# A four-layer transformer kernel: a planner with measured wake-up times, a table of priority offsets, and a bias row with a 128-row operand

## The chip, the cores and the metric

The kernel runs on one core of a Trainium2 chip. The metric is the device time of one execution in microseconds (us). Before the change it is 555.64 us, the median of 3 runs (554.33 to 561.57). The profiled execution has a span of 551.9 us.

## What is computed

Two attention layers and two MLP layers alternate on one sequence of 2048 tokens with 512 channels. Attention has 32 heads of 16 channels and a causal sliding window of 256 tokens.

```
def _A_ref(x, wqkv, wo):                       # H = 32, Dh = 16, W = 256
    q, k, v = split(x @ wqkv)
    scores = q @ k^T * Dh ** -0.5
    mask = (i - j >= 0) & (i - j < W)
    p = softmax(where(mask, scores, -1e9))
    return (p @ v) @ wo
def _B_ref(x, w1, b1, w2, b2):                 # F = 1792
    return gelu(x @ w1 + b1) @ w2 + b2
x = A_x
x = x + _A_ref(layernorm(x), A_wqkv, A_wo)
x = x + _B_ref(layernorm(x), B_w1, B_b1, B_w2, B_b2)
x = x + _A_ref(layernorm(x), A_wqkv, A_wo)
x = x + _B_ref(layernorm(x), B_w1, B_b1, B_w2, B_b2)
```

## The kernel before

**Order.** Nothing is ordered by hand. The builder hands some thousands of operations to a planner, class `_Plan` (L168). `add` (L180) takes an operation's engine, its estimated duration, the names that it reads and writes, a priority (smaller goes first), the PSUM banks that it takes or frees, and, for some, an alternative engine. `run` (L207) then plays the program through on estimated times. At each moment an engine that is free takes the ready operation with the smallest priority whose banks can be had. The order found so is written out as one fixed queue per engine; the waits are added by `_Sched.op` (L62). On the chip every engine works through its queue in that order. If the plan was wrong on when something is ready, the engine stands at it, and what is behind it stands too.

The planner's times have three parts. The first is the duration of each operation, given where it is added: `d_psum`, `d_bf2`, `d_act`, `mm` (L390 to L400) and single numbers. The second is `LAT` (L172), the time from the end of an operation to the moment at which another engine can start on its result; it depends only on the engine that produced it. The third is the time for which a DMA holds its issuing queue on SyncE (`issue`, kept in `geo`), beside the time to its landing. PE pays 98 ns whenever the form of its tiles changes (L294).

**Work.** The two attention layers together give 16 blocks of 256 tokens (`NB`, L845). For each block:
- `layernorm` (L522): statistics on DVE (L530, L532), the reciprocal root on Pool (L534, L537), the normalised row `xn` on DVE (L540), its transposes on PE (L548) and an evacuation (L517 on DVE or L519 on ACT).
- `lnq` and `kv`: projections to Q, K and V. All full-size matmuls go through `pe_group`, so that they share one line, L564.
- `attention`: ten visits. `visit` computes scores into four PSUM banks (L665), in tiles of 32 rows by 64 columns, and ACT takes the exp of each pair of banks (L678). `mask` multiplies the edges of the window with 0 and 1, on DVE (L689) or on Pool (L692). `pv` multiplies with V (L726), four times a block.
- Normalisation, after each `pv`: DVE reduces PSUM to OD (L737). A chain of DMAs on SyncE's queue follows: the denominators go to Dc (L741), DVE takes reciprocals (L744), they go to DRAM (L746) and come back broadcast as Rn (L748); four more copies shift rows of OD (L751). Then OT = OD x Rn on Pool (L754) or DVE (L757). There are 64 such chains with seven DMAs each.
- `outproj`: OT times Wo, then the sum into the stream X (L573).
- `mlp` (L800): the two matmuls of the MLP for a job of two or four tiles of tokens, put in beside later blocks. The bias b1 comes in on DVE (L814) or inside ACT's gelu (L826); ACT reloads its table when it goes between exp and gelu. The bias b2 is the first matmul of each output group (L833): a one-row operand of ones times the row b2, added into PSUM.

**PSUM.** Eight banks are shared by classes of use: scores `sc` take four banks from six possible sets, `o` (projections and the like) one of banks 6 and 7, `od` two banks, `m1` any one.

The last attention block's exps end at about 512 us; the rest of the span is the last jobs of the MLP.

Of the kernel before, what the change touches and what calls it, by code (L numbers as in the profile page):

```python
# [7 lines left out]
ALU = mybir.AluOpType  # L8
# [159 lines left out]
class _Plan:  # L168
# [3 lines left out]
    LAT = {"pe": 230.0, "act": 110.0, "dve": 110.0, "pool": 150.0, "sp": 100.0}  # L172
# [7 lines left out]
    def add(self, eng, fn, dur, reads=(), writes=(), prio=0.0, alloc=None, free=(), after=(), geo=None, table=None, dma=False, alt=(), war=()):  # L180


        i = len(self.nodes)
        deps = set(after)
        for r in reads:
            if r in self.lw:
                deps.add(self.lw[r])
        for w in tuple(writes) + tuple(war):
            if w in self.lw:
                deps.add(self.lw[w])  # L190
            deps.update(self.lr.get(w, ()))
        for r in reads:
            self.lr.setdefault(r, []).append(i)
        for w in writes:
            self.lw[w] = i
            self.lr[w] = []
        deps.discard(i)
        if free and eng == "dve":
            prio -= 1000.0
        self.nodes.append(dict(  # L200
            eng=eng, fn=fn, dur=dur, reads=list(reads), writes=list(writes), prio=prio,
            alloc=alloc, free=tuple(free), deps=deps, geo=geo, table=table, dma=dma,
            alts=((eng, fn, dur, 0.0),) + tuple(alt), done=False,
        ))
        return i

    def run(self):  # L207
# [13 lines left out]
        efree = {e: 0.0 for e in engs}  # L221
        last_geo = [None]
# [16 lines left out]
        while left:  # L239
# [9 lines left out]
            for e in engs:  # L249
                while pend[e] and pend[e][0][0] <= t + 1e-9:  # L250
                    _, i = heapq.heappop(pend[e])
                    for a in nodes[i]["alts"]:
                        if a[0] == e:
                            heapq.heappush(ready[e], (nodes[i]["prio"] + a[3], i))
                if efree[e] > t + 1e-9 or not ready[e]:
                    continue
                skipped = []
                pick = None
                while ready[e]:
                    p, i = heapq.heappop(ready[e])  # L260
                    nd = nodes[i]
                    if nd["done"]:
                        continue
                    if nd["alloc"] is not None:
                        cls, groups = nd["alloc"]
                        got = None
                        for c in self.pools[cls]:
                            if all(bank_free[b] for b in c):
                                got = c
                                break  # L270
                        if got is None:
                            skipped.append((p, i))
                            continue
                        pos = 0
                        for g, k in groups:
                            gmap[g] = got[pos : pos + k]
                            pos += k
                        for b in got:
                            bank_free[b] = False
                    pick = i  # L280
                    break
                for s in skipped:
                    heapq.heappush(ready[e], s)
                if pick is None:
                    continue
                nd = nodes[pick]
                nd["done"] = True
                for a in nd["alts"]:
                    if a[0] == e:
                        nd["eng"], nd["fn"], nd["dur"] = a[:3]  # L290
                dur = nd["dur"]
                if e == "pe":
                    if last_geo[0] is not None and last_geo[0] != nd["geo"]:
                        dur += 98.0  # L294
                    last_geo[0] = nd["geo"]
                if nd["table"] is not None:
                    if last_tab[0] != nd["table"]:
                        dur += 1283.0
                    last_tab[0] = nd["table"]
                nd["start"] = t  # L300
                busy[e] += dur
                end = t + dur
                lat = self.LAT[e]
                if e == "sp":
                    efree[e] = t + nd["geo"]
                else:
                    efree[e] = end
                heapq.heappush(events, (efree[e], pick, None))
                order.append(pick)
                left -= 1  # L310
                for g in nd["free"]:
                    heapq.heappush(events, (end + 90.0, n + seq, gmap[g]))
                    seq += 1
                for s in succ[pick]:
                    same = len(nodes[s]["alts"]) == 1 and nodes[s]["eng"] == e
                    r = end if same and e == "pe" else end + (60.0 if same else lat)
                    if r > rtime[s]:
                        rtime[s] = r
                    indeg[s] -= 1
                    if indeg[s] == 0:  # L320
                        for a in nodes[s]["alts"]:
                            heapq.heappush(pend[a[0]], (rtime[s], s))
                        heapq.heappush(events, (rtime[s], n + seq, None))
                        seq += 1
# [3 lines left out]
        return order  # L328


def bass_interleave_layers__sliding_block__dense_activation_gelu__prompt_kernel(
# [48 lines left out]
    POOL_M = 1120.0  # L380
# [9 lines left out]
    def d_psum(n):  # L390
        return n * 1.042 + 150

    def d_bf2(n):
        return n * 0.52 + 200

    def d_act(n):
        return n * 0.833 + 65
# [4 lines left out]
    with ExitStack() as kctx:  # L402
        S_ = _Sched(nc, kctx)

        def sb(name, shape, dtype=dt.bfloat16):
# [6 lines left out]
        onesb = sb("onesb", [P, P])  # L412
        zerob = sb("zerob", [P, VW])
        b2row = sb("b2row", [P, D])
        b1T = sb("b1T", [P, FC], dt.float32)
# [28 lines left out]
            "sc": [(0, 1, 2, 3), (4, 5, 0, 1), (2, 3, 4, 5), (6, 7, 0, 1), (2, 3, 6, 7), (4, 5, 6, 7)],  # L444
# [35 lines left out]
        add("pool", lambda e, B: e.memset(onesb[:], 1.0), 150, writes=["onesb"])  # L480
        add("pool", lambda e, B: e.memset(Va[:, :, :, Dh:VW], 1.0), 600, writes=["V%d" % i for i in range(VR)])

        for h in range(2):
            add("dve", lambda e, B, h=h: e.memset(ps[:, 4 * h : 4 * h + 4, :], 0.0), 2200, writes=["ps:init%d" % h], prio=-200)
# [30 lines left out]
        def evac(dst, src, n, reads, writes, prio, free=(), after=(), two=False, kind="", boot=False):  # L515

            return add("dve", lambda e, B: e.tensor_copy(dst(B), src(B)), 420 if two else d_psum(n),  # L517
# [5 lines left out]
        def layernorm(tau, layer, dst, dcol, dname, prio):  # L523
# [6 lines left out]
            add("dve", lambda e, B: e.bn_stats(stat6[:, k6, :], X[:, t, :]), 680,  # L530
                reads=["X%d" % t], writes=["st%d" % k6], prio=prio)
            add("dve", lambda e, B: e.bn_aggr(statmv[:, k, :], stat6[:, k6, :]), 150,  # L532
                reads=["st%d" % k6], writes=["mv%d" % k], prio=prio)
            add("pool", lambda e, B: e.tensor_scalar(  # L534
                out=veps[:, k : k + 1], in0=statmv[:, k, 1:2], scalar1=EPS, scalar2=None, op0=ALU.add), 250,
                reads=["mv%d" % k], writes=["ve%d" % k], prio=prio - 500)
            add("pool", lambda e, B: e.tensor_tensor(  # L537
                out=rstd[:, k : k + 1], in0=veps[:, k : k + 1], in1=mhalf[:], op=ALU.pow), 590,
# [3 lines left out]
                op0=ALU.subtract, op1=ALU.mult), 400,  # L542
# [58 lines left out]
        def kv(b, prio, vprio):  # L601
# [3 lines left out]
            for i in range(DC // 2):  # L605
# [5 lines left out]
                    in1=parmask[:, :, None].to_broadcast([P, 2, 512]), op=ALU.mult), d_psum(1024) + 60,  # L611
# [22 lines left out]
        def attention(b, prio):  # L634
# [11 lines left out]
            def visit(g):  # L646
# [12 lines left out]
                def sc(e, B):  # L659
# [11 lines left out]
                    "pe", sc, 512 / 2.4 + 30.0 * len(pieces), reads=rd,  # L671
# [12 lines left out]
            def mask(u, n):  # L684
# [4 lines left out]
                add("dve", lambda e, B: e.tensor_tensor(out=Ew, in0=Ew, in1=Mw, op=ALU.mult), d_bf2(8 * HK * n),  # L689
# [4 lines left out]
            def pv(c):  # L694
# [20 lines left out]
                def fn(e, B):  # L715
# [15 lines left out]
                dpv = 2 * sum(max(q[i][3] - q[i][2] for q in seq if i < len(q)) * HK / 2.4 + 14.0 for i in range(max(len(q) for q in seq)))  # L731
# [11 lines left out]
                    ["Dc%d" % rs], reads=ods, prio=pr - 50, dur=2200.0, issue=580.0)  # L743
                add("dve", lambda e, B: e.reciprocal(Rc[:, rs, :], Dc[:, rs, :]), 330,  # L744
                    reads=["Dc%d" % rs], writes=["Rc%d" % rs], prio=pr - 800)
                dma(lambda e, B: e.dma_start(scr_r[rs].rearrange("h (k n) -> (h k) n", n=32), Rc[:, rs, :]),  # L746
                    ["SR%d" % rs], reads=["Rc%d" % rs], prio=pr - 50, dur=2000.0, issue=490.0)
                dma(lambda e, B: e.dma_start(Rn[:, rs, :], scr_r[rs][:, None, :].to_broadcast([HC, Dh, 2 * P])),  # L748
                    ["Rn%d" % rs], reads=["SR%d" % rs], prio=pr - 50, dur=3200.0, issue=580.0)
                for r in range(RG):  # L750
                    dma(lambda e, B, r=r: e.dma_start(  # L751
                        OD[32 * r + Dh : 32 * r + 2 * Dh, s, 0, :], OD[32 * r : 32 * r + Dh, s, 1, :]),
                        [ods[r]], reads=["Dc%d" % rs], prio=pr, dur=2200.0, issue=350.0)
                add("pool", lambda e, B: e.tensor_tensor(  # L754
                    out=OT[:, bs, c, :], in0=OD[:, s, 0, :], in1=Rn[:, rs, :], op=ALU.mult), 750,
                    reads=ods + ["Rn%d" % rs], writes=["OT%d_%d" % (bs, c)], prio=pr,
                    alt=(("dve", lambda e, B: e.tensor_tensor(  # L757
                        out=OT[:, bs, c, :], in0=OD[:, s, 0, :], in1=Rn[:, rs, :], op=ALU.mult), 420, 0.0),))
# [41 lines left out]
        def mlp(J, live, prio1, prio2):  # L800
# [7 lines left out]
            for f0 in range(0, npre, PG):  # L808
                fcs = range(f0, min(f0 + PG, npre))
                for fc in fcs:  # L810
# [8 lines left out]
                    d_act(M * len(fcs)) + 90, reads=["g%d" % fc for fc in fcs], writes=["g%d" % fc for fc in fcs], prio=prio1,  # L819
                    table="gelu", after=gate_act)  # L820
            for fc in range(npre, FC):
# [6 lines left out]
                    d_act(M) + 90, reads=["ps:" + g, "b1T"], writes=["g%d" % fc], prio=prio1, free=[g],  # L828
                    table="gelu", after=gate_act)
            for i in range(n):  # L830
                tau = tau0 + i
                g = "y%d" % tau
                pe_group(g, [(onesb[0:1, :], b2row[0:1, :], slice(0, 512), True, False)] + [  # L833
# [19 lines left out]

        order = PL.run()
# [46 lines left out]
```

The softmax here doesn't subtract the row's maximum and nothing guards it: scores larger than these inputs give would overflow.

## Time and profile before

| engine | busy, us | share of the span |
|---|---|---|
| TensorE (PE) | 484.1 | 88% |
| ScalarE (ACT) | 423.6 | 77% |
| VectorE (DVE) | 385.9 | 70% |
| GpSimd (POOL) | 271.1 | 49% |

How to read the views. A line of a group or a wait names the engine and the line of the code (L564 is line 564). "A <- B: us, times, longest" in the list of waits says that A's engine was idle until B had finished. In the timeline a row gives start, time, engine and operation, and in brackets the idle time ahead of it with its releaser. PEld is the loading of weights, which runs beside PE; SPq is SyncE's queue, which issues the DMAs. PE's ends are modelled, so PE can be called busy while it drains. The costliest groups are the 320 exps (303.6 us on ACT), the 163 masks on Pool (192.1 us), 448 matmuls of the MLP's second half (120.2 us) and 64 reductions to OD on DVE (77.9 us).

### The profile page before, as it was taken

Reading aid. Unit: us, or ns where it says so; the run is one execution under the profiler, and the core shown is the slowest. Engines: PE = TensorE matmul, PEld = TensorE weight load, DVE = VectorE, ACT = ScalarE, POOL = GpSimd, SP = SyncE. Lnnn points to the kernel's source line nnn. Section 1 sums busy time; section 2 is a strip of 40 time slices with the busy share of each in tenths; the row PEclk is TensorE's granted clock in tenths of the full one; section 3 lists DMA queues with packets and bytes.
Section 4 is the critical chain, followed back from the end, with each engine's and each line's share of the span. In section 5 each row is a group of like instructions: output and inputs, shape, how many; then the busy total and the mean of one; then the engine's idle time right before and its main releaser. Section 6 shows DMA issues by size and latency. Waiting matters only on the chain.

```text
span 551.9 us, 20560 instructions
## 1 busy us (share of the span) xinstructions
PE 484.1 (88%) x9040; PEld 247.1 (45%) x9040; DVE 385.9 (70%) x669; ACT 423.6 (77%) x507; POOL 271.1 (49%) x359
## 2 busy tenths in 40 slices
PE   3895788989878997998998999998999998969997
PEld 2553454545433542545444453445434443434653
DVE  5997986868687666856788686786766675863331
ACT  2788798889877894798869987589757996788542
POOL 6575664646584335643566457562553344532010
PEclk9998799999979997998999999999999999979999
DMA  8901111010111011100111101110111102110100
GB/s 275 297 17 41 43 27 40 23 34 20 36 45 33 14 25 38 37 24 11 37 35 33 30 14 42 34 29 15 45 53 43 32 9 61 45 45 25 51 20 30
DMA packets 37131, 24.93 MB, mean 45 GB/s; under 512 B 16305, under 2 KB 36530, under 8 KB 37042
## 3 DMA queue, kind: packets, MB, share of 16 engines
q1 hardware_dynamic: 37042, 23.62, 14.6%
q8 instruction: 71, 1.16, 0.9%
q14 instruction: 18, 0.15, 0.1%
HBM read 16.26 MB, written 2.62 MB: 34 GB/s over the span
## 4 chain that ended last, share of the span: by engine, by line
PE 39%; DMA 18%; DVE 18%; SPq 12%; ACT 9%; issue 3%; POOL 1%; DVEq 0%; POOLq 0%
PE ps L564 30%; SPq L751 9%; DMA Dc<-OD 7%; DMA Rn<-scr_r 6%; ACT E L678 5%; DMA scr_r<-Rc 5%; DVE OD L737 4%; PE ps L665 4%; PE ps L726 3%; DVE KT L608 2%; DVE E L689 2%; DVE X L573 2%; ACT gT L826 1%; SPq L748 1%; PE ps L548 1%
## 5 line engine op out<-in xcount | busy, mean ns | idle before, releaser
L678 ACT ACTIVATE E<-ps 128x1024 bf16<-128x1024 f32 x320 | 303.6, 1039 | 65.4 <-PE ps L665 65.0
L692 POOL TENSOR_TENSOR E<-E,mask 128x512 bf16<-128x512 bf16 x163 | 192.1, 1187 | 147.1 <-ACT E L678 147.1
L564 PE MATMUL ps<-xnTB,W_sb 128*128 128x512 bf16 (+1 forms) x560 | 114.5, 339 | 7.9 <-DVE gT L814 3.9
L564 PE MATMUL ps<-W_sb,gT 128*128 128x512 bf16 x448 | 120.2, 383 | 0.0
L737 DVE TENSOR_REDUCE OD<-ps 128x512 f32<-128x1024 f32 x64 | 77.9, 1217 | 14.9 <-PE ps L726 14.4
L665 PE MATMUL ps<-QT,KT 32*64 32x320 bf16 (+4 forms) x3072 | 69.8, 265 | 15.5 <-ACT E L678 9.4
L564 PE MATMUL ps<-xnTA,Wqkv_sb 128*128 128x256 bf16 x512 | 70.5, 281 | 6.3 <-DVE xnTA L517 1.7
L564 PEld LDWEIGHTS ps<-xnTB,W_sb 128*128 128x128 bf16 x560 | 50.2, 98 | 51.1 <-DVE gT L814 6.8
L573 DVE TENSOR_TENSOR X<-X,ps 128x512 bf16<-128x512 bf16 x64 | 43.2, 676 | 38.7 <-PE ps L564 38.6
L826 ACT ACTIVATE gT<-ps,b1T 128x512 bf16<-128x512 f32 (+1 forms) x92 | 50.4, 584 | 18.6 <-PE ps L564 18.4
L689 DVE TENSOR_TENSOR E<-E,mask 128x512 bf16<-128x512 bf16 x93 | 53.0, 572 | 14.4 <-ACT E L678 13.7
L665 PEld LDWEIGHTS ps<-QT,KT 32*64 32x64 bf16 x3072 | 29.0, 104 | 69.7 <-ACT E L678 36.0
L564 PEld LDWEIGHTS ps<-W_sb,gT 128*128 128x128 bf16 x448 | 37.7, 98 | 45.2 <-issue 14.7
L726 PE MATMUL ps<-E,Va 64*17 64x192 bf16 (+3 forms) x3840 | 52.2, 238 | 6.5 <-DVE E L689 2.7
L564 PEld LDWEIGHTS ps<-xnTA,Wqkv_sb 128*128 128x128 bf16 x512 | 46.3, 100 | 24.0 <-issue 3.3
L726 PEld LDWEIGHTS ps<-E,Va 64*17 64x17 bf16 x3840 | 42.5, 87 | 29.6 <-issue 13.0
L754 POOL TENSOR_TENSOR OT<-OD,Rn 128x256 bf16<-128x256 f32 x34 | 25.2, 741 | 61.9 <-DMA Rn<-scr_r 56.8
L564 PE MATMUL ps<-Wo_sb,OT 128*128 128x512 bf16 x128 | 36.2, 419 | 9.3 <-POOL OT L754 6.9
L608 DVE TENSOR_TENSOR KT<-ps,parmask 128x1024 bf16<-128x1024 f32 x32 | 38.6, 1213 | 6.8 <-PE ps L564 6.6
L530 DVE BATCH_NORM_STATS2 stat<-X 128x6 f32<-128x512 bf16 x64 | 42.8, 679 | 0.5
L744 DVE RECIPROCAL Rc<-Dc 64x32 f32<-64x32 f32 x64 | 21.6, 338 | 28.6 <-DMA Dc<-OD 28.5
L564 PE MATMUL ps<-Wqkv_sb,xnTA 128*128 128x512 bf16 x128 | 35.4, 393 | 5.1 <-DVE KT L608 3.3
(46 smaller groups left out, 360.8 us busy)
## 6 DMA issues: line engine op xcount, KB each, us to landing
Rn<-scr_r SPq DMA_DIRECT2D x64, 128.0 KB
OD<-OD SPq DMA_DIRECT2D x256, 16.0 KB
W_sb<-in_B_w_dram SPq DMA_DIRECT2D x2, 1792.0 KB
out_dram<-X SPq DMA_DIRECT2D x16, 128.0 KB
Wqkv_sb<-in_A_wqkv_dram SPq DMA_DIRECT2D x3, 512.0 KB
X<-in_A_x_dram SPq DMA_DIRECT2D x1, 1024.0 KB
Dc<-OD SPq DMA_DIRECT2D x64, 8.0 KB
scr_r<-Rc SPq DMA_DIRECT2D x64, 8.0 KB
```

What stands on the lines that cost most here:

```text
L530: add("dve", lambda e, B: e.bn_stats(stat6[:, k6, :], X[:, t, :]), 680, reads=["X%d" % t], writes=["st%d" % k6], prio=prio)
L564: r = e.matmul(ps[:, B[g][0], cols], lhsT, rhs, start=st, stop=sp)
L573: add("dve", lambda e, B: e.tensor_tensor(out=X[:, t, :], in0=X[:, t, :], in1=ps[:, B[g][0], :], op=ALU.add), d_psum(512), reads=["X%d" % ...
L608: add("dve", lambda e, B, g=g, i=i: e.tensor_tensor(out=KT[:, kb, :, 2 * i : 2 * i + 2, :].rearrange("p a c q -> p a (c q)"), in0=ps[:, B[ ...
L665: x = e.matmul(ps[HK * h : HK * h + HK, bk[r], o : o + n], KT[rows, kb, par, c, j * P + HK * h : j * P + HK * h + HK], QT[rows, c, q + HK ...
L678: a = (add("act", lambda e, B, g_=g_, gi=gi: e.activation(E[:, 2 * gi : 2 * gi + 2, e0 : e0 + 512], ps[:, B[g_][0] : B[g_][0] + 2, :], AF. ...
L689: add("dve", lambda e, B: e.tensor_tensor(out=Ew, in0=Ew, in1=Mw, op=ALU.mult), d_bf2(8 * HK * n), reads=["E%d%s" % (es, x) for es in ess ...
L692: alt=(("pool", lambda e, B: e.tensor_tensor(out=Ew, in0=Ew, in1=Mw, op=ALU.mult), POOL_M * n, POOL_H),))
L726: x = e.matmul(ps[32 * r : 32 * r + VW, B[g][half], par * 256 + q_lo * HK : par * 256 + q_hi * HK], lhsT, rhs, start=(pi == 0), stop=(pi = ...
L737: add("dve", lambda e, B: e.tensor_reduce(out=OD[:, s, :, :].rearrange("p a q -> p (a q)"), in_=ps[:, B[g][0] : B[g][0] + 2, :].rearrange( ...
L751: dma(lambda e, B, r=r: e.dma_start(OD[32 * r + Dh : 32 * r + 2 * Dh, s, 0, :], OD[32 * r : 32 * r + Dh, s, 1, :]), [ods[r]], reads=["Dc%d ...
L826: gelu_last[0] = add("act", lambda e, B, g=g, fc=fc: e.activation(gT[:, fc, 0:M], ps[:, B[g][0], 0:M], AF.Gelu_apprx_tanh, bias=b1T[:, fc ...
```

## The change

The change is meant to make the planner's picture of the chip truer, and then to search for a better order with it. It has these parts:

1. **Latencies.** `LAT` is split into `TAIL`, by the engine that ends, and `WAKE`, by the engine that starts. Between two operations on PE or two on ACT nothing is added.
2. **Durations and DMA issue times** are set anew all over the kernel. For DVE and Pool they become shorter, because the tail is now counted apart; for DMA issues they become longer (a copy of OD: 350 to 610 ns).
3. **Tile forms on PE.** A change of form costs 57 ns when it goes to full-size tiles, 98 ns when it leaves them, and 5 ns between two small forms.
4. **Port lock.** Operations marked `lock` (all of Pool, and on DVE the masks, xn and OT) wait, in the plan, until the other engine's marked operation has ended.
5. **`_TUNE`.** A table of offsets, which `tune` adds to the priorities by group (engine and name of what is written) and by block (200 units of priority each).
6. **Banks for scores.** Of the six sets, the three without banks 6 and 7 remain.
7. **The b2 row.** The one-row operand becomes a 128-row one: `one0` has ones in row 0 and zeros elsewhere, and b2row's other rows are set to 0.

```diff
-    LAT = {"pe": 230.0, "act": 110.0, "dve": 110.0, "pool": 150.0, "sp": 100.0}
+    TAIL = {"pe": 100.0, "act": 130.0, "dve": 93.0, "pool": 48.0, "sp": 0.0}
+    WAKE = {"pe": 134.0, "act": 24.0, "dve": 24.0, "pool": 70.0, "sp": 16.0}
...
+    def tune(self, table, span):
+        for nd in self.nodes:
+            name = nd["writes"][0].translate({ord(c): None for c in "0123456789_"})
+            t = table.get(nd["eng"] + " " + name)
+            pr = nd["prio"]
+            if nd["free"] and nd["eng"] == "dve":
+                pr += 1000
+            if name == "Rc":
+                pr += 800
+            if name in ("ve", "rs"):
+                pr += 500
+            if t is not None and pr >= -90:
+                nd["prio"] += t.get(int((pr + 60) // span), 0)
...
+                if nd["lock"] and e in port:
+                    dur += max(0.0, port["pool" if e == "dve" else "dve"] - t)
+                    port[e] = t + dur
                 if e == "pe":
                     if last_geo[0] is not None and last_geo[0] != nd["geo"]:
-                        dur += 98.0
+                        dur += 57.0 if nd["geo"] == "f" else 98.0 if last_geo[0] == "f" else 5.0
...
-                    heapq.heappush(events, (end + 90.0, n + seq, gmap[g]))
+                    heapq.heappush(events, (end + self.TAIL[e] + self.WAKE["pe"], n + seq, gmap[g]))
...
-                    same = len(nodes[s]["alts"]) == 1 and nodes[s]["eng"] == e
-                    r = end if same and e == "pe" else end + (60.0 if same else lat)
+                    d = nodes[s]["eng"]
+                    r = end if d == e and (e == "pe" or e == "act") else end + self.TAIL[e] + self.WAKE[d]
...
+_TUNE = {
+    'act Ea': {2: -35},
+    'dve Ed': {4: -506},
+    'dve X': {4: -383, 13: 214},
...
+    'pe ps:k': {0: -108, 1: 225, 4: -106, 5: -274, 6: 176, 7: -89, 8: -281, 9: 65, 12: 60, 13: 194, 14: 214, 15: 259},
+    'pe ps:m': {2: -756, 3: -143, 5: 75, 7: -25, 11: -96, 15: -67},
...
+    'pe ps:sa': {0: -529, 1: -336, 2: -331, 3: -104, 9: 27, 10: 19, 11: 19, 12: 14},
...
+    'pe ps:y': {5: 96, 7: 1207, 9: 137, 11: 219, 13: 254, 15: 305},
...
+}
...
-    POOL_M = 1120.0
+    POOL_M = 1115.0
...
     def d_psum(n):
-        return n * 1.042 + 150
+        return n * 1.042 + 64
     def d_bf2(n):
-        return n * 0.52 + 200
+        return n * 0.52 + 75
     def d_act(n):
-        return n * 0.833 + 65
+        return n * 0.833 + 50
...
-            "sc": [(0, 1, 2, 3), (4, 5, 0, 1), (2, 3, 4, 5), (6, 7, 0, 1), (2, 3, 6, 7), (4, 5, 6, 7)],
+            "sc": [(0, 1, 2, 3), (4, 5, 0, 1), (2, 3, 4, 5)],
...
-        add("pool", lambda e, B: e.memset(onesb[:], 1.0), 150, writes=["onesb"])
+        add("pool", lambda e, B: e.memset(one0[:], 0.0), 150, writes=["onesb"])
+        add("pool", lambda e, B: e.memset(one0[0:1, :], 1.0), 150, writes=["onesb"])
+        add("pool", lambda e, B: e.memset(b2row[:], 0.0), 300, writes=["b2row"])
...
-                    ["Dc%d" % rs], reads=ods, prio=pr - 50, dur=2200.0, issue=580.0)
+                    ["Dc%d" % rs], reads=ods, prio=pr - 50, dur=1800.0, issue=658.0)
...
-                    ["SR%d" % rs], reads=["Rc%d" % rs], prio=pr - 50, dur=2000.0, issue=490.0)
+                    ["SR%d" % rs], reads=["Rc%d" % rs], prio=pr - 50, dur=1745.0, issue=535.0)
...
-                    ["Rn%d" % rs], reads=["SR%d" % rs], prio=pr - 50, dur=3200.0, issue=580.0)
+                    ["Rn%d" % rs], reads=["SR%d" % rs], prio=pr - 50, dur=2740.0, issue=690.0)
...
-                        [ods[r]], reads=["Dc%d" % rs], prio=pr, dur=2200.0, issue=350.0)
+                        [ods[r]], reads=["Dc%d" % rs], prio=pr, dur=2000.0, issue=610.0)
...
-                pe_group(g, [(onesb[0:1, :], b2row[0:1, :], slice(0, 512), True, False)] + [
+                pe_group(g, [(one0[:], b2row[:], slice(0, 512), True, False)] + [
...
+        PL.tune(_TUNE, 200.0)
         order = PL.run()
```

## The prediction

> **What bounds the kernel now.** I read the page's busy shares first, then the table by stretches, the list of waits (the DMA queue's own too), and last the timeline around the longest waits.
>
> ```profile
> PE 484.1 (88%) x9040; PEld 247.1 (45%) x9040; DVE 385.9 (70%) x669; ACT 423.6 (77%) x507; POOL 271.1 (49%) x359
> ...
> PE 39%; DMA 18%; DVE 18%; SPq 12%; ACT 9%; issue 3%; POOL 1%; DVEq 0%; POOLq 0%
> ```
>
> No engine is full over the span, and the chain of waits passes through all of them; DMA plus its issuing queue (SPq) hold 30% of it. That is a kernel bound by the order of its work. The stretches say where:
>
> ```profile
> 50.00:83.00 33.00, 24.84 (x718) 14.46 (x713) 29.74 (x54) 28.82 (x34) 22.02 (x29) 0.84 0.14 37
> ...
> 281.00:314.00 33.00, 30.82 (x485) 15.73 (x469) 24.57 (x45) 26.59 (x33) 18.99 (x25) 1.00 0.12 34
> ...
> 347.00:380.00 33.00, 30.94 (x484) 14.88 (x484) 24.17 (x42) 26.42 (x33) 14.88 (x21) 1.00 0.10 28
> ```
>
> The columns are busy us of PE, PEld, DVE, ACT and POOL, then the granted clock. Early, DVE is the fullest (29.7 of 33); from 281 us on PE is, at some 31 of 33, and ACT has 6 us of slack. So PE's order decides most of the loop. The loop of attention blocks runs from about 20 us to 512 us. In it the timeline of PE shows 53.3 us idle; 19 patches of 0.9 us or more make 25.8 us of that. ACT is idle for 88.4 us in the same time.
>
> ```profile
> ACT E L678 <- PE ps L665: 65.0, 47, 5.5
> POOL OT L754 <- DMA Rn<-scr_r: 56.8, 23, 8.7
> ```
>
> ACT's exps wait 65 us for score matmuls (L665). The longest patch shows why:
>
> ```profile
> 204.99 0.82 PE L564 MATMUL ps<-W_sb,gT 128*128 128x512 bf16 x3
> ...
> 205.81 0.80 PE L726 MATMUL ps<-E,Va 64*17 64x256 bf16 x64
> 206.19 0.64 SPq L748 DMA_DIRECT2D Rn<-scr_r  x1
> ...
> 208.99 0.72 POOL L754 TENSOR_TENSOR OT<-OD,Rn 128x256 bf16<-128x256 f32 x1 [3.23 <-DMA Rn<-scr_r]
> ...
> 209.77 1.89 PE L564 MATMUL ps<-Wo_sb,OT 128*128 128x512 bf16 x4 [3.16 <-POOL OT L754]
> ...
> 212.31 1.02 ACT L678 ACTIVATE E<-ps 128x1024 bf16<-128x1024 f32 x1 [5.19 <-PE ps L665]
> ```
>
> The out-projection stands in PE's fixed order ahead of the next scores. Its operand OT needs the reciprocals Rn, which arrive late. PE stands for 3.16 us, and ACT, behind PE, for 5.19 us. The clock then adds to it (columns as above):
>
> ```profile
> 155.20:162.00 6.80, 4.11 (x146) 2.21 (x154) 6.21 (x13) 6.42 (x8) 5.56 (x9) 0.68 0.13 36
> ...
> 206.40:213.20 6.80, 3.64 (x53) 1.13 (x32) 4.16 (x8) 1.61 (x2) 3.33 (x4) 0.68 0.11 31
> ...
> 486.30:493.10 6.80, 3.11 (x122) 1.78 (x123) 4.16 (x8) 6.77 (x8) 2.97 (x3) 0.68 0.19 57
> ```
>
> Where PE was busy for under two thirds, its clock fell to 0.68 on the mean. Over the span the granted clock is 0.969, so 0.031 x 551.9 = 17.1 us of full-speed PE time is lost.
>
> **What the Trainium skill says.** SBUF — State Buffer, "SBUF: two separate sides": DVE and GpSimd share one port pair as an exclusive lock, and the loser blocks until the other ends. The trace agrees: the DVE mask starting at 257.04 us took 1.14 us (median 0.425 us) beside a Pool mask that ran from 256.74 to 257.90 us. TensorE: Matmul & The Clock Gate, "What's actually happening": the array drops to half clock after an idle window of about 3.4 us and returns after a busy one. The trace agrees as far as the slow stretches go with a thin PE. TensorEngine Tiling (Array Packing), "Key Properties": changing the tiling mode drains the array; the trace puts a number on it below.
>
> **Part 1, the planner's costs.** They change no instruction, only the order in each queue. What matters is where the old ones miss the trace. SPq: OD<-OD issues have a median of 585 ns, planned 350; the seven issues of one normalisation take 4 x 585 + 609 + 530 + 642 = 4.12 us, planned 3.05. That is 1.07 us too little for each of the 64 normalisations, in a queue that runs in order: exactly the late Rn above. The new costs (4 x 610 + 658 + 535 + 690 = 4.32) fit. Wake-ups: scores ending at 253.30 us release an exp at 253.38, 0.08 us against 0.23 planned; an ACT copy ending at 255.75 us releases PE at 256.05, 0.30 us against 0.11. DVE: two statistics in a row end 1.28 us after the first began, so they follow each other by 1.28 - 0.68 = 0.60 us, while 0.68 plus 0.11 was planned. The lock, planned at nothing, costs DVE 93 x (572 - 425) + 64 x (531 - 406) + 30 x (534 - 425) ns = 24.9 us (mean less median of masks, xn and OT), most of it beside PE work from 281 us on, but in the open early on. A plan with these numbers would not put an out-projection ahead of scores while its Rn is still on the way. Bounds on what it recovers: nothing, or all 25.8 us of the large PE patches. The small patches, some 0.3 us each, are wake-ups and stay. I take 0.6, since DMA landings vary (Rn 2.6 to 3.9 us in the chain) and no fixed order meets them all: **15.5 us**. Denser work also keeps the clock up: bounds 0 and 17.1 us, I take a third, **5.7 us**, since some thin stretches early are DVE's doing.
>
> **Part 2, the priority table.** It shifts ready work by group and by block, so it too changes only order. On its own it could spread or crowd the same waits; I put it inside the 0.6 above rather than count it twice.
>
> **Part 3, score banks.** Scores (four banks a visit) may no longer use banks 6 and 7. Three pairs still rotate: while the second exp of a visit runs (1.04 us), the next scores (0.43 us) can fill the two pairs already read. Bounds: 0, or, if a tenth of the 160 visits come to wait 1.4 us more (65.0/47, the mean wait now), 16 x 1.4 = 22 us. What queues behind a score group that finds no bank is all of PE's later work. I take 0, because banks 6 and 7 also carry the projections, which in turn are blocked less.
>
> **Part 4, the b2 row.** The 32 matmuls with a one-row operand become 128-row ones:
>
> ```profile
> 544.82 0.59 PE L564 MATMUL ps<-W_sb,gT 128*128 128x512 bf16 x2
> 545.34 0.39 PE L564 MATMUL ps<-b2row,onesb 1*128 1x512 bf16 x1
> 545.66 1.04 PE L564 MATMUL ps<-W_sb,gT 128*128 128x512 bf16 x4
> ```
>
> Four equal matmuls take 1.04 us, one 0.38, so they follow each other by (1.04 - 0.38)/3 = 0.22 us. The second of the first row began at 544.82 + 0.59 - 0.38 = 545.03; the b2 matmul follows 0.31 us later, and the next 0.32 us after that. Extra: 0.09 + 0.10 = 0.19 us, x 32 = 6.1 us of PE time; where a score group follows anyway, one half of it stays. The four in the tail, which only PE fills from 532 us on, give 0.8 us whole; of the 28 in the loop (5.3 us) I take 0.7: **4.5 us** in all, between 0.8 and 6.1. The added memsets (two small ones and the b2 row's) run on Pool before 16 us, where it is busy 8.8 of 16, and the b2 row is first used at 92.87 us: nothing.
>
> **Sum.** 15.5 + 5.7 + 4.5 = 25.7 us: 555.6 - 25.7 = 529.9, say **530 us**.
>
> **The rivals.** (a) The plan bites fully: large patches, clock and b2 all come back, 25.8 + 17.1 + 6.1 = 49 us, **507 us**. For it: ACT (423.6 us busy) and PE would still fit. Against: ACT needs scores through one in-order PE, and of the 53.3 us idle only 25.8 are large patches, of many causes. (b) New stalls replace the old: the order is right on the mean but the DMA's spread and clock make others as large, and only b2 counts: **551 us**. For it: the 19 large patches have eleven different releasers, so no single cause goes away. (c) Slower: the score banks bind and the exps wait as bounded above: 555.6 - 4.5 + 22 = **573 us**. For it: ACT's largest wait already is scores. Against: the plan sees the banks exactly; only the times are estimates.
>
> **How the numbers follow.** Forecast 0.55, (a) 0.15, (b) 0.17, (c) 0.13. Faster by over 2% (under 544.5) is the forecast and (a): 0.70; within 2% is (b): 0.17; slower is (c): 0.13. The range runs from 505, just under (a), to 562, which holds (b) with its spread and leaves (c) out.
>
> **What would show it.** Right: exps waiting for scores well below 65 us; PE idle in the loop below 40 us and no patch of 3 us behind OT; a clock above 0.975; b2 rows with 128*128 following their neighbours by 0.22 us. Wrong: exps waiting more than 65 us with PE no fuller (the banks), or the same idle time under other releasers (b). If PE is denser and the span isn't shorter, the loop isn't PE's, and the reading by stretches fails.

## The result, and the profile after

The changed kernel takes 539.38 us (median of 4, 536.08 to 542.12), against 558.61 us for the kernel before in the same rounds. The ratio is 0.966, with a 95% interval of 0.956 to 0.976: faster by 3.4%. The forecast was 530 us with a range of 505 to 562; it holds, but the gain is smaller than forecast. In later rounds, beside other kernels, the changed kernel had 537.09 us and a ratio of 0.962 (0.956 to 0.967). Executions come in a faster and a slower state, and ratios are formed from the faster ones alone, so a ratio need not be the quotient of the medians given with it.

The busy shares and the chain of waits of the changed kernel:

```profile
PE 475.4 (88%) x9040; PEld 246.5 (46%) x9040; DVE 381.8 (71%) x660; ACT 426.7 (79%) x511; POOL 275.4 (51%) x366
...
PE 33%; DMA 23%; SPq 15%; DVE 14%; ACT 9%; issue 3%; POOL 2%; DVEq 0%; POOLq 0%
```

The work of PE is the same 9,040 matmuls; it lies in less time. DMA and its issuing queue hold more of the chain than before (38% against 30%), so the normalisation did not leave the critical path.

The table by stretches (time, busy us of PE, PEld, DVE, ACT, POOL, then the clock). First the loop of attention blocks of the kernel before, from its first exp to the end of its last:

```profile
20.00:512.10 492.10, 437.30 (x8675) 218.97 (x8675) 360.73 (x625) 402.13 (x469) 258.29 (x308) 0.97 0.13 35
512.10:551.90 39.80, 36.03 (x282) 20.87 (x281) 11.93 (x21) 15.64 (x31) 2.72 (x5) 1.00 0.11 34
```

and the same of the changed kernel:

```profile
22.50:498.60 476.10, 429.26 (x8674) 218.02 (x8672) 355.79 (x610) 404.40 (x470) 259.23 (x307) 0.97 0.13 35
498.60:537.70 39.10, 34.58 (x280) 20.67 (x278) 10.55 (x20) 15.31 (x32) 3.66 (x6) 0.99 0.11 35
```

The loop became 16.0 us shorter, the head 2.5 us longer, the tail 0.7 us shorter. Of the 16.0 us, PE's busy time gave 8.0 (437.30 to 429.26) and its idle time 8.0 (492.10 - 437.30 = 54.8 to 476.10 - 429.26 = 46.8).

The list of waits of the changed kernel:

```profile
POOL OT L800 <- DMA Rn<-scr_r: 88.0, 34, 12.8
...
ACT E L724 <- PE ps L711: 38.6, 52, 2.4
...
PE ps L610 <- POOL OT L800: 12.0, 9, 1.7
ACT E L724 <- PE ps L772: 11.7, 4, 5.8
```

Exps wait for scores for 38.6 us instead of 65.0, and never over 2.4 us; four more waits, put down to the matmuls with V, make 11.7 us, so the exps wait 50.3 us for PE in all. But Pool waits longer for Rn (88.0 against 56.8), and PE waits for Pool's OT for 12.0 us (6.9 before). The longest wait of an exp is now this (timeline):

```profile
213.90 0.72 POOL L800 TENSOR_TENSOR OT<-OD,Rn 128x256 bf16<-128x256 f32 x1 [2.44 <-DMA Rn<-scr_r]
...
214.01 0.34 DVE L790 RECIPROCAL Rc<-Dc 64x32 f32<-64x32 f32 x1 [3.31 <-DMA Dc<-OD]
...
214.84 0.66 DVE L563 CAST QT<-ps 128x512 bf16<-128x512 f32 x1
...
215.55 1.17 PE L610 MATMUL ps<-xnTA,Wqkv_sb 128*128 128x256 bf16 x8 [2.91 <-DVE QT L563]
...
218.63 1.25 PE L772 MATMUL ps<-E,Va 64*17 64x256 bf16 x64
...
219.97 1.02 ACT L724 ACTIVATE E<-ps 128x1024 bf16<-128x1024 f32 x1 [5.78 <-PE ps L772]
```

DVE stands for 3.31 us at a reciprocal whose operand a DMA brings, and the cast of Q behind it starts late. PE stands for 2.91 us at the cast, and the exp, which waits for the matmuls with V further on in PE's order, stands for 5.78 us. The kind of stall that the prediction showed is still there.

The clock, first at the three times at which it was 0.68 before (other work lies there now), then in an early stretch:

```profile
155.20:162.00 6.80, 6.39 (x164) 2.71 (x161) 6.60 (x10) 6.10 (x8) 6.04 (x6) 1.00 0.05 12
206.40:213.20 6.80, 6.05 (x134) 2.58 (x111) 4.26 (x6) 5.71 (x8) 3.88 (x4) 1.00 0.11 30
486.30:493.10 6.80, 6.80 (x53) 3.06 (x50) 0.85 (x2) 6.45 (x9) 0.73 (x1) 1.00 0.10 29
34.00:40.80 6.80, 6.22 (x123) 3.12 (x124) 4.61 (x7) 5.79 (x7) 5.57 (x8) 0.61 0.07 15
```

In the first three PE is busy for 6.05 to 6.80 of 6.80 us, and the clock is whole. In the fourth it is 0.61 although PE is called busy for 6.22 us: at the low clock the matmuls themselves take longer (16 score matmuls of one shape 0.65 us at 37.44 us, 0.42 us at 207.79 us), so the busy time of a slow stretch doesn't say how much work it holds. The loss has moved to the start of the loop: up to 83 us the clock was 0.92 and is 0.86, from there to the loop's end it was 0.97 and is 0.99. Over the span the mean clock went from 0.969 to 0.977 in the two profiled runs, so the loss from 17.1 to 0.023 x 537.7 = 12.4 us. Finally the b2 row:

```profile
527.96 0.38 PE L610 MATMUL ps<-b2row,one 128*128 128x512 bf16 x1
528.18 3.19 PE L610 MATMUL ps<-W_sb,gT 128*128 128x512 bf16 x14
```

The next matmul follows 528.18 - 527.96 = 0.22 us later, as any other does.

### The profile page after: what moved, and what is told of

Read it like the earlier page. It is cut to its first block, busy times and chain, and to the rows that moved or that the text cites. A ratio compares the mean times of both kernels' runs of the same rounds, so it can differ in the third digit from the quotient of the medians.

```text
span 537.7 us, 20551 instructions
## 1 busy us (share of the span) xinstructions
PE 475.4 (88%) x9040; PEld 246.5 (46%) x9040; DVE 381.8 (71%) x660; ACT 426.7 (79%) x511; POOL 275.4 (51%) x366
## 4 chain that ended last, share of the span: by engine, by line
PE 33%; DMA 23%; SPq 15%; DVE 14%; ACT 9%; issue 3%; POOL 2%; DVEq 0%; POOLq 0%
PE ps L610 26%; DMA Dc<-OD 12%; SPq L797 10%; ACT E L724 7%; DMA Rn<-scr_r 5%; DMA scr_r<-Rc 5%; DVE OD L783 4%; PE ps L772 3%; PE ps L711 3%; SPq L794 2%; DVE KT L654 2%; SPq L792 2%; DVE X L619 1%; PE ps L594 1%; DVE E L735 1%
## 5 line engine op out<-in xcount | busy, mean ns | idle before, releaser
L724 ACT ACTIVATE E<-ps 128x1024 bf16<-128x1024 f32 x320 | 305.2, 1033 | 51.2 <-PE ps L711 38.6
L738 POOL TENSOR_TENSOR E<-E,mask 128x512 bf16<-128x512 bf16 x161 | 189.5, 1187 | 98.9 <-ACT E L724 98.2
L610 PE MATMUL ps<-W_sb,gT 128*128 128x512 bf16 x448 | 123.2, 382 | 0.0
L610 PE MATMUL ps<-xnTB,W_sb 128*128 128x512 bf16 (+1 forms) x560 | 111.8, 339 | 4.9 <-DVE gT L860 4.0
L800 POOL TENSOR_TENSOR OT<-OD,Rn 128x256 bf16<-128x256 f32 x41 | 31.1, 759 | 92.8 <-DMA Rn<-scr_r 88.0
L610 PE MATMUL ps<-xnTA,Wqkv_sb 128*128 128x256 bf16 x512 | 71.7, 283 | 7.6 <-DVE QT L563 3.8
L735 DVE TENSOR_TENSOR E<-E,mask 128x512 bf16<-128x512 bf16 x95 | 55.6, 587 | 11.4 <-ACT E L724 10.6
L610 PEld LDWEIGHTS ps<-W_sb,gT 128*128 128x128 bf16 x448 | 38.9, 98 | 40.9 <-issue 9.2
L610 PE MATMUL ps<-Wo_sb,OT 128*128 128x512 bf16 x128 | 33.1, 388 | 15.2 <-POOL OT L800 12.0
L594 PE MATMUL ps<-ident,xn 128*128 128x128 bf16 x256 | 26.2, 228 | 16.4 <-DVE xn L586 10.8
```

The costliest lines, as they stand in the source:

```text
L610: r = e.matmul(ps[:, B[g][0], cols], lhsT, rhs, start=st, stop=sp)
L724: a = (add("act", lambda e, B, g_=g_, gi=gi: e.activation(E[:, 2 * gi : 2 * gi + 2, e0 : e0 + 512], ps[:, B[g_][0] : B[g_][0] + 2, :], AF. ...
L738: alt=(("pool", lambda e, B: e.tensor_tensor(out=Ew, in0=Ew, in1=Mw, op=ALU.mult), POOL_M * n, POOL_H),))
```

## The experiments

Theory: the planner's costs were wrong, above all for the DMA issues; with true ones the large waits of PE go, and a 128-row b2 saves its drain. Rivals: the table alone makes the gain; no single cost matters; the drain is hidden.

### Each part alone

The first kernel is the one before with the b2 row alone (item 7 of the change, Part 4 of the prediction). Its queues are not quite the old ones, because the planner orders the added memsets too.

```diff
-        add("pool", lambda e, B: e.memset(onesb[:], 1.0), 150, writes=["onesb"])
+        add("pool", lambda e, B: e.memset(one0[:], 0.0), 150, writes=["onesb"])
+        add("pool", lambda e, B: e.memset(one0[0:1, :], 1.0), 150, writes=["onesb"])
+        add("pool", lambda e, B: e.memset(b2row[:], 0.0), 300, writes=["b2row"])
...
-                pe_group(g, [(onesb[0:1, :], b2row[0:1, :], slice(0, 512), True, False)] + [
+                pe_group(g, [(one0[:], b2row[:], slice(0, 512), True, False)] + [
```

> The kernel before with the 128-row b2 operand alone; the planner's costs are the old ones, and its order changes only where the extra memsets move something. My theory (the one-row matmul costs 0.19 us of PE time more): 4 to 5 us under before, ratio 0.991 to 0.993, and the b2 group's neighbours 0.22 us apart. Rival (the drain is hidden because PE waits elsewhere): no difference, ratio 1.00.

Measured: 546.51 us, ratio 0.990 (0.985 to 0.995). The interval holds the forecast and leaves out "no difference", but queues have moved, so the price of the edit comes from a better pair below.

The second has all the new costs and nothing else. Against the changed kernel (the memsets of the b2 operands go back too, and are left out here):

```diff
-            "sc": [(0, 1, 2, 3), (4, 5, 0, 1), (2, 3, 4, 5)],
+            "sc": [(0, 1, 2, 3), (4, 5, 0, 1), (2, 3, 4, 5), (6, 7, 0, 1), (2, 3, 6, 7), (4, 5, 6, 7)],
...
-                pe_group(g, [(one0[:], b2row[:], slice(0, 512), True, False)] + [
+                pe_group(g, [(onesb[0:1, :], b2row[0:1, :], slice(0, 512), True, False)] + [
...
-        PL.tune(_TUNE, 200.0)
```

> The changed kernel's planner costs alone (latencies, durations, DMA issue times, tile forms, port lock), without the table, with the six score sets and with the one-row b2 operand. My theory (truer costs take out most of the large waits): 15 to 20 us under before, ratio about 0.966 to 0.973. Rival (a truer plan finds no better order by itself; the table does it): ratio 0.99 to 1.01.

Measured: 558.55 us, ratio 1.011 (1.007 to 1.014). My theory falls: true costs alone make the kernel slower, by 1.1%. The third is the changed kernel without the call of `tune`:

```diff
-        PL.tune(_TUNE, 200.0)
```

> The changed kernel without the table of offsets alone. My theory: most of the gain stays, ratio to before 0.965 to 0.98. Rival (the table carries the gain): ratio 0.985 to 1.01, with exps waiting for scores 55 us or more.

Measured: 562.85 us, ratio 1.018 (1.014 to 1.022). Its list of waits:

```profile
POOL E L738 <- ACT E L724: 152.9, 92, 10.5
ACT E L724 <- PE ps L711: 72.8, 55, 5.6
...
POOL OT L800 <- DMA Rn<-scr_r: 40.1, 21, 4.3
```

Pool waits for Rn less than in the kernel before (40.1 against 56.8 us, longest 4.3 against 8.7), as I had said of true costs; but OT, on both engines, waits longer for the shifted copies of OD (20.6 against 6.9 us). The exps wait for scores more (72.8 against 65.0 us). The reason may be that the priorities had not been set for these costs; that isn't shown. This kernel has the 128-row b2 and the three score sets on top of the second one, and is 4 us slower than it, not faster. Without a table, then, the three sets, or the new order that they bring, cost more than the b2 row gains. The table is needed; whether the true costs are needed beside it, these runs don't say.

### The price of the b2 row

Here the one-row operand is put back into the changed kernel. The queues of PE, ACT, DVE and SyncE then hold the same operations in the same order, and only memsets on Pool at the start differ.

```diff
-                pe_group(g, [(one0[:], b2row[:], slice(0, 512), True, False)] + [
+                pe_group(g, [(onesb[0:1, :], b2row[0:1, :], slice(0, 512), True, False)] + [
```

> The changed kernel with the one-row b2 operand put back; the order of PE, ACT and DVE is the same as in the changed kernel, so this prices the b2 edit by itself. My theory: 4 to 6 us over the changed kernel (about 544). Rival (hidden): the same 539.

Measured: 536.49 us, ratio 0.972 (0.967 to 0.977). Against the 539.38 us of the changed kernel this would be a saving, but that one was timed in other rounds, beside a kernel before of 558.61 us and not 554.08. The ratios (0.972 and 0.966) say the opposite of the times. So both were run in one set of rounds:

> The changed kernel once more, as the yardstick beside the next three. All theories: ratio to before 0.96 to 0.975.

> The changed kernel with the one-row b2 operand, once more, beside the changed kernel itself. The queues of PE, ACT, DVE and SyncE are the same as in the changed kernel, two memsets on Pool apart. If the drain of the one-row matmul is on the path: 4 to 6 us over the changed kernel. If it is hidden: within 2 us of it.

Measured: 537.09 us (ratio 0.962, 0.956 to 0.967) with 128 rows and 542.47 us (0.972, 0.967 to 0.977) with one row. The edit is worth about 5.4 us. The six runs of one kernel spread by up to 10 us and the ratios' intervals just touch, so by my estimate this is good to some 3 us; the b2 row alone, above, and the two ratios 0.972 and 0.966 also give 3 to 6 us. The timeline of the one-row kernel in its tail shows the gaps:

```profile
530.59 2.97 PE L608 MATMUL ps<-W_sb,gT 128*128 128x512 bf16 x13 [0.16 <-issue]
533.49 0.39 PE L608 MATMUL ps<-b2row,onesb 1*128 1x512 bf16 x1
533.80 2.55 PE L608 MATMUL ps<-W_sb,gT 128*128 128x512 bf16 x11
```

The next matmul comes 0.31 us later instead of 0.22. The last one ahead began at 530.59 + 2.97 - 0.38 = 533.18, so the b2 row comes 0.31 us after it as well. The extra is 0.18 to 0.19 us, or about 6 us for 32, of which about 5.4 reach the end. The runs show the gap; that it is a drain of the array is the prediction's reading of it.

### Does a table need true costs?

For the next kernels I searched tables of my own: from an empty one, change offsets at random and keep what doesn't end the plan later, with about as many trials for each table. The first kernel has the old costs throughout (what stands behind # in this fence and in later ones is a remark, not code):

```diff
 (against the kernel before)
-            "sc": [(0, 1, 2, 3), (4, 5, 0, 1), (2, 3, 4, 5), (6, 7, 0, 1), (2, 3, 6, 7), (4, 5, 6, 7)],
+            "sc": [(0, 1, 2, 3), (4, 5, 0, 1), (2, 3, 4, 5)],
...
-                pe_group(g, [(onesb[0:1, :], b2row[0:1, :], slice(0, 512), True, False)] + [
+                pe_group(g, [(one0[:], b2row[:], slice(0, 512), True, False)] + [
...
+        PL.tune(_TUNE, 200.0)      # a table searched against the old costs
         order = PL.run()
```

> The planner with the old costs (latencies, durations, DMA issue times, no lock) but with the three score sets, the 128-row b2 operand and a table of offsets that was searched from an empty one against the old costs' own plan. Theory now (a search pays only as far as the costs are true): half of the gain or less, ratio to before 0.98 to 1.0. Rival (any table that was searched finds a denser order, true costs are not needed): as good as the next kernel, 0.96 to 0.975.

Measured: 549.43 us, ratio 0.986 (0.983 to 0.990). The b2 row alone had given 0.990 (0.985 to 0.995). The second has the new costs:

```diff
 (against the changed kernel)
-_TUNE = {    # the changed kernel's table
+_TUNE = {    # a table searched from an empty one against the same costs
```

> The changed kernel with another table: searched from an empty one against the new costs, with as many trials as the kernel with the old costs had. If the gain comes from search on true costs and not from these offsets in particular: the changed kernel's time within 6 us, ratio to before 0.96 to 0.98. If the changed kernel's offsets hold something special that the plan doesn't show: ratio 0.985 or more.

Measured: 535.37 us, ratio 0.960 (0.955 to 0.966). So the changed kernel's offsets hold nothing special: another table found on the same costs gives the same time. The one found on the old costs gives hardly anything beyond the b2 row. In these runs search and true costs are needed together.

### Which of the costs?

The costs were split in two: those of the normalisation's DMAs (issue and landing), and all the others. The first kernel has the old DMA costs and every other new one:

```diff
 (against the changed kernel; and a table of its own)
-                    ["Dc%d" % rs], reads=ods, prio=pr - 50, dur=1800.0, issue=658.0)
+                    ["Dc%d" % rs], reads=ods, prio=pr - 50, dur=2200.0, issue=580.0)
...
-                    ["SR%d" % rs], reads=["Rc%d" % rs], prio=pr - 50, dur=1745.0, issue=535.0)
+                    ["SR%d" % rs], reads=["Rc%d" % rs], prio=pr - 50, dur=2000.0, issue=490.0)
...
-                    ["Rn%d" % rs], reads=["SR%d" % rs], prio=pr - 50, dur=2740.0, issue=690.0)
+                    ["Rn%d" % rs], reads=["SR%d" % rs], prio=pr - 50, dur=3200.0, issue=580.0)
...
-                        [ods[r]], reads=["Dc%d" % rs], prio=pr, dur=2000.0, issue=610.0)
+                        [ods[r]], reads=["Dc%d" % rs], prio=pr, dur=2200.0, issue=350.0)
```

> The changed kernel with the old DMA issue and landing times of the normalisation chain and every other new cost, and a table searched from an empty one against these costs with as many trials as before. If the DMA costs are what makes the plan true (the prediction's named cause): ratio to before 0.975 to 0.99. If latencies, durations and the lock are: 0.96 to 0.972.

Measured: 555.20 us, ratio 1.002 (1.000 to 1.005), slower than either forecast: not even the b2 row's gain is left. The second is its converse. It is the old-costs kernel above with these four lines the other way round, and a table searched for it.

> The converse: the old latencies and durations, no lock and no new tile costs, but the new DMA issue and landing times, with the three score sets, the 128-row b2 operand and a table searched in the same way. If the DMA costs are what matters: 0.96 to 0.972. If the others are: 0.98 to 0.99, like the kernel with all costs old.

Measured: 535.24 us, ratio 0.960 (0.953 to 0.967), as good as with all costs new. In busy shares and waits the kernel with the old DMA costs reads

```profile
PE 478.5 (87%) x9040; PEld 246.3 (45%) x9040; DVE 385.0 (70%) x659; ACT 425.2 (77%) x506; POOL 282.6 (51%) x372
...
PE 30%; DMA 29%; DVE 17%; SPq 17%; issue 3%; ACT 2%; POOL 1%; DVEq 0%; POOLq 0%
...
POOL OT L814 <- DMA Rn<-scr_r: 68.2, 27, 6.2
ACT E L738 <- PE ps L725: 59.7, 56, 5.2
...
DVE OT L817 <- DMA Rn<-scr_r: 29.5, 18, 3.7
```

and the one with the new DMA costs and all others old

```profile
PE 471.0 (89%) x9040; PEld 243.4 (46%) x9040; DVE 384.9 (73%) x658; ACT 422.1 (80%) x506; POOL 282.3 (53%) x373
...
PE 28%; DMA 22%; SPq 18%; DVE 16%; ACT 10%; issue 3%; POOL 1%; DVEq 0%; POOLq 0%
...
POOL OT L810 <- DMA Rn<-scr_r: 46.6, 27, 4.2
ACT E L734 <- PE ps L721: 46.5, 44, 4.0
...
DVE OT L813 <- DMA Rn<-scr_r: 22.9, 14, 5.6
```

With untrue DMA costs OT stands for Rn for 68.2 us on Pool and 29.5 on DVE, against 46.6 and 22.9 with true ones, DMA holds 29% of the chain instead of 22%, and the exps wait 13 us longer. But the two kernels differ in all their costs and in their tables, so the lines show how they differ and not what did it; and Pool's wait for Rn is no measure of the time, for in the changed kernel it is 88.0 us at a ratio of 0.966. The spans of these profiles are 552.5 and 528.0 us; the second is one of the fastest runs of its kernel, whose median is 535.24. Of the 24.5 us between them, PE's busy time makes 7.5 and its idle time 17.0. The mean clock is 0.972 against 0.989. That is 15.5 against 5.8 us of PE time lost, enough for the 7.5. In the loop, from the first exp to the end of the last, PE's idle patches of 0.9 us or more sum to 32.4 us (21 of them) with the old DMA costs and to 19.5 us (15) with the new ones, the smaller ones to 23.8 and 21.0 us.

The four kernels side by side, ratios to the kernel before, all with the 128-row b2 and three score sets:

| table searched on | old latencies, durations, no lock | new ones |
|---|---|---|
| old DMA costs | 0.986 (0.983 to 0.990) | 1.002 (1.000 to 1.005) |
| new DMA costs | 0.960 (0.953 to 0.967) | 0.960 (0.955 to 0.966) |

The row decides. Within the lower row the column does nothing. Why it does harm in the upper one stays open; with one table for each set of costs it may be the luck of the search. Such luck hardly explains the rows: the changed kernel and the four searches on true DMA costs (these two and the two of the next section) all came out between 0.960 and 0.967, both searches on the old ones at 0.986 or more.

### Score banks, and spread

The changed kernel with all six score sets, and a table searched for them:

```diff
-            "sc": [(0, 1, 2, 3), (4, 5, 0, 1), (2, 3, 4, 5)],
+            "sc": [(0, 1, 2, 3), (4, 5, 0, 1), (2, 3, 4, 5), (6, 7, 0, 1), (2, 3, 6, 7), (4, 5, 6, 7)],
```

> The changed kernel with all six score sets and a table searched from an empty one for them in the same way. If leaving out banks 6 and 7 costs or gains nothing once the table is searched (the prediction's value): 0.957 to 0.967, like the three-set kernel searched in the same way. If the three sets are worth something: 0.97 or more; if they cost something: under 0.955.

Measured: 536.21 us, ratio 0.964 (0.957 to 0.970), against 0.960 (0.955 to 0.966) for three sets. Leaving out banks 6 and 7 is worth nothing that can be told apart.

The last kernel is the changed one with a table searched for another aim:

```diff
-_TUNE = {    # the changed kernel's table
+_TUNE = {    # searched for the mean end of its queues under varied landings and a clock that halves
```

> The changed kernel's costs with a table that was searched not for the earliest end of the plan but for the mean end of its fixed queues under landing times that vary by about a fifth and a PE clock that halves after a thin stretch. If the gap between plan and chip is this spread: 3 to 6 us under the changed kernel, ratio to before 0.948 to 0.957. If the gap has other causes: 0.96 to 0.965.

Measured: 535.73 us, ratio 0.967 (0.963 to 0.971): above both forecasts, and no gain. A plan made for spread, as I modelled it, is no better. No kernel here is clearly faster than the changed one.

## Why the prediction was right, and where it failed

**Direction and range: right, with some luck.** But for the b2 row it is the same operations, in another order and in part on another engine, that take less time, so order was the bound. But the largest term of the sum came out of other waits than those it was worked out from, and the range was wide enough for that.

**The b2 row: right in mechanism and about in size.** 4.5 us were forecast, about 5.4 measured. The 0.19 us read from the trace of before was the right price. The part of it on the path was taken as 0.7 in the loop; it may be more, but the spread of the runs doesn't tell 4.5 from 5.4.

**The order and the clock: a third of the forecast did not come.** The two terms were 15.5 + 5.7 = 21.2 us. Measured is 556.61 - 537.09 = 19.5 us in all, less 5.4 for b2: 14.1 us. The clock term fits: 17.1 - 12.4 = 4.7 us in the profiled runs, and, by the mean clocks of the faster runs in the later rounds (0.966 before, 0.981 after), 19.0 - 10.3 = 8.7 us. That leaves 5 to 9 us for the order. The step that failed is "0.6 of the 25.8 us of large PE patches". The timeline of PE in the changed loop still has 19 patches of 0.9 us or more, and they sum to 27.7 us. What shrank are the small ones, from 27.5 to 16.9 us (57 patches became 42), and these the prediction had called wake-ups that stay. This is no accident of one table: in the profiles of the kernel with the new DMA costs alone and of the one searched for spread, the small patches sum to 21.0 and 18.6 us and the large ones to 19.5 and 25.2. (Most of the other kept traces lack about a hundred matmul records and can't be read so.)

**The marks.** Met: exps waiting for scores well below 65 us (38.6, or 50.3 with the four waits behind the matmuls with V), the clock above 0.975 (0.977, narrowly; the faster runs of the changed kernel have 0.971 to 0.990), the b2 rows at 0.22 us, and no patch of 3 us behind OT (the longest is 2.8 us, behind an OT on DVE). Missed: PE idle in the loop below 40 us (53.3 became 44.6 in the timeline). And the mark on OT was met in its letter only: PE's wait for Pool's OT grew from 6.9 to 12.0 us.

**Part 1, the claim that truer costs order the work better: wrong as it stood.** Alone they cost 1.1% (0.7 to 1.4). The prediction said that the table might spread or crowd the same waits and put it inside the same term; in fact without it there is no gain at all.

**Part 1, the claim that the DMA costs are what was wrong: right; that it is the issue time, not shown.** The prediction singled out SPq's 4.12 us against 3.05 planned. The two-by-two table shows that with true DMA costs the wake-up times, DVE durations and the port lock, listed beside them, change nothing. But issue and landing times were changed together; which of the two it is wasn't tried. The prediction's own example speaks for caution. This is SyncE's queue ahead of the late Rn, which was issued at 206.19 us, in the kernel before:

```profile
199.70 3.03 SPq L751 DMA_DIRECT2D OD<-OD  x3
202.84 0.53 SPq L746 DMA_DIRECT2D scr_r<-Rc  x1
```

Three copies hold the queue for 3.03 us, where the old costs have 3 x 0.35 = 1.05 and the new ones 1.83; then 3.35 us pass from the issue of the reciprocals to that of Rn, where they have a landing of 2.00 and 1.75. The sums are 6.38 us measured, 3.05 with the old costs and 3.58 with the new ones. So the new costs cover 0.5 of the 3.3 us by which this Rn was late; the rest was in neither, and "exactly the late Rn" was too much said. How a true DMA cost reaches the end is not shown either. PE waits for OT for nearly the same time in the last pair of profiles (12.2 us with the old DMA costs, 11.4 with the new), and the large patches that are fewer there have many releasers.

**One reading was wrong without effect.** For two statistics in a row the prediction gave 0.68 plus 0.11 us as planned. They don't depend on each other, and `run` frees an engine at the end of an operation, so 0.68 was planned, against 0.60 in the trace.

**Part 3, the score banks: right** at nothing, once a table has been searched; without a table they may cost, as the third kernel showed. Rival (c) falls. Rival (b), that only b2 counts, falls with 0.962 against 0.990 for b2 alone, though its argument, new stalls as large as the old, is what the large patches show. Rival (a) falls with the large patches.

## What to carry to other kernels

When a fixed order is planned from costs, look first at the costs on the queue which nothing can overtake: here an issuing queue that was planned at three quarters of its real time, and whose landing times were changed with it. Correct costs by themselves didn't improve this greedy plan, whose priorities had been set for the old ones; search the priorities again, and only then judge the costs. And price an edit beside its counterpart in the same rounds: a b2 row worth 5.4 us looked like a loss of 3 us when the two were timed apart.

## What was not expected of the hardware

That a matmul with one row among full ones costs 0.09 to 0.10 us on each side was readable in the trace; that most of it, about 5.4 of some 6 us, would reach the end was not expected, with PE idle for a tenth of the loop. Also not expected was how far the clock moves. Between the profiles with old and with new DMA costs PE's idle time differs by 17.0 us, and the mean clock is 0.972 against 0.989; the same 9,040 matmuls are busy for 7.5 us less. The order isn't all of it: the kernel with the new DMA costs, with its queues fixed, had runs from 528.63 us at a mean clock of 0.990 to 536.23 us at 0.983.
